# Local attention with global keys and a SwiGLU block: the written-out order of all steps replaced by another order

## Chip, core and metric

One core of one Trainium2 chip. The metric is the device time of one execution in microseconds, the median of several runs.

## The reference

Attention over `B, H, S, D = 4, 8, 768, 64`: a key is kept when it is one of the first 8 (global) or lies 0 to 95 positions back (local); a bias of a slope per head times the distance is added, then softmax. The result, 3072 tokens by 512, goes through a SwiGLU block.

```python
scores = scale * np.matmul(q, k.transpose(0, 1, 3, 2)) + bias
a = softmax(np.where(is_global | is_local, scores, -1e9))
x = (a @ v).transpose(0, 2, 1, 3).reshape(3072, 512)
g = x @ w_gate                       # 512 x 1536
out = (g * sigmoid(g) * (x @ w_val)) @ w_out
```

## The kernel before, in words

One Python string, `ORDER` (lines 67 to 147), names every step of the program with its arguments; the last lines of the kernel walk through it and call one function per step. There is no scheduler: each engine and each DMA queue executes its own steps in the order of the string, and semaphores hold a step until its inputs are there and its buffer is free. So a step's place in the string matters only against the steps of the same engine or queue, and for which buffers and PSUM banks it gets.

The 3072 tokens are four batches of two halves, eight token blocks `t = 2 * batch + half` of 384 tokens. Head pairs are numbered 0 to 3 (`hp`), two pairs make a group `g`. The steps that the text speaks of:

- **Software loads, issued by POOL** (lines 276 to 358), in a row: `Lh.i.half.h0.h1` heads of `k` (i = 0) or `q` (i = 1) of batch 0; `Lv.b.c` a chunk of 120 keys of the values (48 for c = 6); `Lr.b.i.h` one head of `k` or `q` as rows; `L4.i.h0` four heads; `Lw.which.n.g` half of a third of `w_gate` (0) or `w_val` (1), 256 KB; `Lo.g` a third of `w_out`, 512 KB; `Ld.P.half` distances for the masks. `Z.b.P` and `kz.P` are POOL memsets in the same row; `Z.b` clears parts of the value buffer, which two batches share in turn, and so waits for the last reader of the batch whose buffer it takes.
- **SP's queue**: a few early loads (`Lf.S`, `Li`, `Ld.S`); `D.b.hp.i` (line 483) transposes one head pair's rows by DMA into `kN` (i = 0) or `qT` (i = 1); `G.b...S` copies the global values; and the copies out that `e.t.i` issues (line 753).
- **PE**: `T` and `U` transposes, `b` and `B` bias products with a diagonal slope matrix, `C` and `c.b.g.half.up` scores (line 520), `V` and `W` weighted values (586, 614), `w` sums of weights (597, 630), `g.t.f` and `v.t.f` the four matmuls of one 128-wide slice `f` of gate and value product (line 693, both), `o.t.i.part` a quarter of one 128-token output tile (line 734; 723 for the last two tiles), `fill.n` matmuls whose result nothing uses (394).
- **ACT and DVE**: `cast`, `k`, `q`, `kw`, `qw`, `K` move and spread transposed keys and queries (the last letter is the engine); `E` and `x` exponentials (ACT); `M` masks from distances (ACT); `m` masking (DVE); `X` a copy of the values with the halves of the partitions swapped; `n` copies weighted values out of PSUM (ACT); `i`, `j`, `r`, `p` invert, spread and apply the sums, `p` writing the block's `xT`; `t` tanh (ACT), `s` and `h` the SwiGLU products (DVE, line 709); `e` scales an output tile by 0.5 on ACT (752) and issues its copy out.

Buffers that are handed on: eight PSUM banks, dealt in the order of the string from those released earliest (lines 236 to 259); two `osb` tiles for the copies out, so that `e` waits for the copy out two before it; two value buffers; two `kN`.

Batch 1's pairs 0 and 1 are transposed on PE (`U`), its pairs 2 and 3 by four `D` steps; batches 2 and 3 by eight `D` each.

Of the kernel before, what the change touches and what calls it, by code (L numbers as in the profile page):

```python
# [809 lines left out]
```

## Time and profile before

| | us |
|---|---|
| median of 3 runs (237.11 to 238.77) | 238.52 |
| the profiled execution's own time | 237.59 |
| its span, first to last instruction | 235.8 |
| PE busy in the span | 229.6 |
| DVE busy | 169.5 |
| ACT busy | 116.3 |
| POOL busy (issuing software loads, above all) | 79.8 |

The clock that was granted is 1.000. A row of the timeline has the start in the span, the length, the engine, the line of the kernel and the operation, with the output and input names; in brackets stands how long the engine sat idle ahead of it and what ended that. In the list of DMA issues the last number is the time from issue to landing. A row of the chain has start, length and what ran.

### The profile page before, as it was taken

To read this page: it belongs to the slowest core of one execution; us is meant where nothing else is said; L and a number is where in the kernel's file an instruction comes from. 1 tells how busy PE (TensorE), PEld (TensorE's weight loads), DVE (VectorE), ACT (ScalarE), POOL (GpSimd) and SP (SyncE) were. 2 spreads that over 40 slices of the span, in tenths; PEclk is the share of its full clock that TensorE was granted. 3 is DMA by queue.
4 is the path that set the end of the run, shared out by engine and by line. 5 is a ranking of instruction groups with operands and counts; after the bars stand their busy time and mean duration, and the time that the engine had idled before them with its cause. 6 is when DMAs were issued, how large, how long until landed. Compare 5 with 4: busy or idle time off the path is not lost.

```text
span 235.8 us, 6107 instructions
## 1 busy us (share of the span) xinstructions
PE 229.6 (97%) x2515; PEld 133.6 (57%) x2515; DVE 169.5 (72%) x389; ACT 116.3 (49%) x219; POOL 79.8 (34%) x113
## 2 busy tenths in 40 slices
PE   7999899998999999999999999999999999999998
PEld 4466566554455666655556556565555565555446
DVE  3998898869466789969979998984495876542200
ACT  3688847546842734357858674440424341311321
POOL 8976759731581599788100000000000000000000
DMA  6999999999999899999996311010012000010332
GB/s 171 194 180 188 204 197 178 171 140 122 188 145 184 190 161 135 124 153 153 143 204 152 39 49 47 0 47 0 3 44 89 0 3 0 1 44 3 135 129 93
DMA packets 88324, 25.97 MB, mean 110 GB/s; under 512 B 78048, under 2 KB 85256, under 8 KB 88296
## 3 DMA queue, kind: packets, MB, share of 16 engines
q0 software_dynamic: 67120, 14.25, 79.2%
q1 hardware_dynamic: 20488, 10.74, 23.4%
q10 hardware_dynamic: 688, 0.59, 0.7%
q8 instruction: 19, 0.31, 0.6%
q14 instruction: 9, 0.07, 0.1%
HBM read 28.93 MB, written 6.29 MB: 149 GB/s over the span
## 4 chain that ended last, share of the span: by engine, by line
PE 66%; DMA 23%; POOL 7%; ACT 3%; issue 1%; POOLq 0%; ACTq 0%
PE banks L693 39%; PE banks L734 20%; DMA kst<-in_k_dram 9%; DMA wo<-in_moe_w_out_dram 8%; DMA wv<-in_moe_w_val_dram 4%; DMA out_dram<-osb 2%; POOL vS L292 2%; PE banks L520 2%; PE banks L614 2%; PE banks L723 1%; PE banks L394 1%; POOL k L284 1%; POOL q L284 1%; POOL wg L351 1%; PE banks L630 1%
## 5 line engine op out<-in xcount | busy, mean ns | idle before, releaser
L699 ACT ACTIVATE th<-banks 128x384 f32<-128x384 f32 x96 | 44.3, 494 | 59.4 <-PE banks L693 56.4
L693 PE MATMUL banks<-xT,wv 128*128 128x384 f16 x384 | 71.4, 326 | 0.0
L693 PE MATMUL banks<-xT,wg 128*128 128x384 f16 x384 | 71.2, 326 | 0.1
L709 DVE TENSOR_TENSOR hT<-banks,sl 128x384 f16<-128x384 f32 x96 | 50.8, 552 | 21.2 <-PE banks L693 19.8
L734 PE MATMUL banks<-wo,hT 128*128 128x512 f16 x276 | 65.8, 379 | 0.0
L703 DVE SCALAR_TENSOR_TENSOR sl<-th,banks 128x384 f32<-128x384 f32 x96 | 50.1, 547 | 17.3 <-ACT th L699 16.7
L693 PEld LDWEIGHTS <-wv 128*128 128x128 f16 x384 | 37.3, 98 | 26.3
L693 PEld LDWEIGHTS <-wg 128*128 128x128 f16 x384 | 36.7, 98 | 25.6 <-issue 0.6
L734 PEld LDWEIGHTS <-hT 128*128 128x128 f16 x276 | 26.3, 98 | 28.2 <-issue 0.2
L530 ACT ACTIVATE at<-banks 128x976 f16<-128x976 f32 (+3 forms) x28 | 25.5, 958 | 12.1 <-PE banks L520 12.1
L292 POOL DMA_DIRECT2D vS<-in_v_dram x28 | 25.2, 908 | 9.8 <-DMA vS<-in_v_dram 6.7
L752 ACT ACTIVATE osb<-banks 128x512 f32<-128x512 f32 x23 | 13.5, 599 | 23.3 <-PE banks L734 14.6
L344 POOL DMA_DIRECT2D qst<-in_q_dram x20 | 17.2, 860 | 8.8 <-DMA wo<-in_moe_w_out_dram 4.1
L539 DVE TENSOR_TENSOR at<-at,masks 128x976 f16<-128x976 f16 (+3 forms) x26 | 15.7, 643 | 4.1 <-ACT at L530 4.1
L663 DVE STREAM_TRANSPOSE rb<-dR 128x384 f32<-128x384 f32 x32 | 16.7, 553 | 2.8 <-ACT dR L659 2.7
L344 POOL DMA_DIRECT2D kst<-in_k_dram x20 | 16.7, 841 | 2.6 <-DMA vS<-in_v_dram 1.1
L520 PE MATMUL banks<-qT,kT 64*64 64x152 f16 (+9 forms) x456 | 9.2, 214 | 1.6 <-DMA qT<-qst 1.6
L520 PEld LDWEIGHTS <-kT 64*64 64x64 f16 x456 | 7.2, 107 | 5.8 <-issue 4.8
L678 DVE TENSOR_TENSOR xT<-banks,rb 128x384 f16<-128x384 f32 x16 | 8.4, 546 | 1.3 <-PE banks L614 1.2
L319 ACT COPY vX<-vS 64x1792 f16<-64x1792 f16 (+2 forms) x6 | 7.3, 1220 | 3.3 <-DMA kst<-in_k_dram 3.2
L637 ACT COPY ns<-banks 128x768 f32<-128x768 f32 x6 | 4.7, 807 | 7.9 <-PE banks L614 7.9
L614 PEld LDWEIGHTS <-vS 64*64 64x64 f16 x228 | 6.6, 107 | 2.6 <-issue 2.1
(77 smaller groups left out, 165.2 us busy)
## 6 DMA issues: line engine op xcount, KB each, us to landing
out_dram<-osb SPq DMA_DIRECT2D x23, 256.0 KB, 2.1
vS<-in_v_dram POOLq DMA_DIRECT2D x24, 120.0 KB, 7.7
qst<-in_q_dram POOLq DMA_DIRECT2D x20, 96.0 KB, 7.2
kst<-in_k_dram POOLq DMA_DIRECT2D x20, 96.0 KB, 6.7
wg<-in_moe_w_gate_dram POOLq DMA_DIRECT2D x6, 256.0 KB, 7.3
wv<-in_moe_w_val_dram POOLq DMA_DIRECT2D x6, 256.0 KB, 8.2
wo<-in_moe_w_out_dram POOLq DMA_DIRECT2D x3, 512.0 KB, 18.2
k<-in_k_dram POOLq DMA_DIRECT2D x3, 192.0 KB, 5.7
```

The source lines that it names most:

```text
L292: nc.gpsimd.dma_start(out=v_of(b)[r0:r0 + n, c, heads(g), :], in_=v[b, heads(g), KC * c:KC * c + n, :].rearrange("h p d -> p h d"))
L344: nc.gpsimd.dma_start(out=rows_of(i, b, h // 2)[:, :, h % 2, :], in_=KQ[i][b, h].rearrange("(t p) d -> p t d", p=128))
L520: nc.tensor.matmul(sc[64 * r:64 * r + 64, hi, col:col + n], lhsT=kTs[2 * g + r][d, k0:k0 + 64], rhs=qTs[b, 2 * g + r][d, q0:q0 + n], start ...
L530: nc.scalar.activation(out=at[:, :, 0:w], in_=sc[:, :, 0:w], func=AF.Exp, scale=scale)
L539: ENG[e].tensor_mul(a2, a2, masks[:, 2 * g:2 * g + 2, x:x + w])
L663: nc.vector.transpose(rb.rearrange("p (n i) -> p n i", i=32), rbs[b, half][:, g, r].unsqueeze(2).broadcast_to([128, TB // 32, 32]))
L693: nc.tensor.matmul(gv[t, f, which][:, 0:TB], lhsT=w[:, c, 128 * f:128 * f + 128], rhs=xTs[t][:, c, :], start=(c == 0), stop=(c == NC - 1))
L699: nc.scalar.activation(out=th, in_=gv[t, f, 0][:, 0:TB], func=AF.Tanh, scale=0.5)
L703: nc.vector.scalar_tensor_tensor(out=sl, in0=gv[t, f, "t"], scalar=1.0, in1=gv[t, f, 0][:, 0:TB], op0=AluOp.add, op1=AluOp.mult)
L709: nc.vector.tensor_mul(hTs[t][:, f, :], gv[t, f, 1][:, 0:TB], gv[t, f, "s"])
L734: nc.tensor.matmul(ops_t[t, i], lhsT=hTs[t][:, f, 128 * i:128 * i + 128], rhs=wo[:, f, :], start=(f == 0), stop=(f == NFF - 1))
L752: nc.scalar.mul(out=osb, in_=ops, mul=0.5)
```

## The change

All steps stand in another order. The first fifteen software loads are the same ones in the same sequence, but for `Ld.P.1`, which stands two places earlier; from the sixteenth on the sequence differs. The scores (`c`) and DMA transposes (`D`) of batch 1, and nearly everything behind them, have other places among the products. Some copies move between ACT and DVE, three of the six `n` steps are gone, and the fillers are 5 + 10 at the start and 7 + 2 + 4 at the end instead of 11 + 5 and 23. No function is changed. Of the 80 lines on each side those that hold the steps spoken of:

```diff
--- before
+++ after
 ORDER = """
-Lf.A.1.1 Z.0.P pre Lf.S.0.1 Lf.A.1.0 cast.1.1.V Li cast.1.0.V fill.11 fill.5 Z.1.P kz.P sl.1 sl.7
-sl.6 cast.0.1.A T.1.0.1 Lh.0.0.4.8 T.1.0.0 Ld.S.2 sl.2 sl.0 sl.3 b.1.0 k.1.0.A Lh.1.0.4.8 Lf.S.0.0
-Lh.1.1.4.8 sl.5 T.0.0.1 b.1.1 q.1.0.V pk Ld.P.1 cast.0.0.A C.1.0 T.0.0.0 Lv.0.0 sl.4 Lh.0.1.0.4
...
-k.0.1.A q.1.1.V E.2.1 T.2.1.0 T.0.1.1 k.1.1.V q.2.1.V w.0.0.1 Lv.0.4 Lv.0.5 k.2.1.A B.1.1.0 q.0.1.A
-B.1.1.1 i.0.0.1 Lw.0.2.0 r.0.1.0.0 k.3.1.A V.1 c.0.0.1.0 p.0.0.0.1.V V.0 c.0.1.1.1 p.0.0.0.0.V V.2
-M.1.1 x.0.0.1.0 r.0.1.0.1 c.0.1.1.0 c.0.0.1.1 V.3 p.0.1.0.0.V p.0.1.0.1.V x.0.0.1.1 m.0.0.1.0.V
...
-t.0.11 s.0.11 p.0.1.1.1.V Lw.0.1.0 v.0.10 h.0.9 h.0.11 U.1.1 U.0.1 U.0.0 U.1.0 qw.1.A t.0.10 D.1.3.0
...
-g.1.11 kw.1.A t.1.0 D.1.2.1 g.1.3 s.1.2 h.0.10 v.1.2 v.1.10 s.1.0 h.1.0 h.1.2 Lr.1.0.4 v.1.3 t.1.3
-g.1.1 Lr.1.0.5 t.1.11 g.1.9 g.1.6 D.1.2.0 D.1.3.1 Z.2.P Lw.1.1.1 t.1.1 s.1.11 h.1.10 s.1.3 t.1.6
...
-s.1.9 c.1.0.0.1 Lv.1.0 s.1.8 s.0.6 x.1.0.0.0 x.1.0.0.1 Lv.1.2 h.1.1 h.1.8 Lo.0 g.0.7 g.1.7 g.0.5
-t.0.5 g.1.5 v.0.5 v.1.9 v.1.6 K.1.3 s.0.5 Lv.1.5 h.1.9 g.0.4 v.0.6 Lo.1 Lv.1.6 t.1.7 t.0.4 h.0.5
-h.1.6 c.1.0.1.0 v.1.7 t.0.7 Lo.2 s.1.7 s.0.4 h.0.6 Lv.1.4 Lv.1.3 t.1.5 x.1.0.1.0 s.1.5 g.1.4 Lv.1.1
...
-Lr.2.0.5 v.1.5 h.0.7 h.1.4 c.1.1.0.1 c.1.1.0.0 c.1.1.1.1 G.1.1.7.S x.1.1.0.1 x.1.1.0.0 h.1.5 o.0.0.0
-o.1.0.0 Lr.2.1.5 c.1.0.1.1 D.2.2.0 m.1.0.0.0.V c.1.1.1.0 x.1.1.1.1 M.3.0 Lr.2.1.7 Lr.2.0.6 o.0.0.1
...
-o.1.0.2 i.1.0 j.1.0.A o.1.2.1 o.0.2.1 i.1.1 Lr.2.0.2 Lr.2.1.4 r.1.1.0.0 Lr.2.0.1 e.0.0 o.1.0.3
-o.1.2.2 o.1.2.3 W.1.0.0 e.1.0 D.2.3.1 D.2.2.1 W.1.0.1 r.1.0.0.1 o.0.1.1 o.0.1.2 p.1.0.0.1.V
-p.1.1.0.0.V o.0.1.3 r.1.1.0.1 e.1.2 j.1.1.A r.1.0.0.0 p.1.1.0.1.V p.1.0.0.0.V o.0.2.2 o.0.2.3 g.2.3
-e.0.2 t.2.3 D.2.3.0 W.1.1.0 W.1.1.1 n.1.0.1 r.1.1.1.1 r.1.0.1.0 g.2.4 g.2.6 r.1.0.1.1 g.2.7 t.2.4
-v.2.6 Z.3.P s.2.3 s.2.4 n.1.1.1 g.2.1 g.2.2 t.2.6 t.2.2 Lr.3.0.6 Lr.3.1.6 p.1.0.1.1.V v.2.3 v.2.4
...
-e.6.0 o.7.1.2 h.7.9 o.7.1.3 o.7.2.0 e.6.1 o.7.0.1 e.7.1 o.7.0.2 o.7.0.3 o.7.2.1 o.7.2.2 o.7.2.3
-fill.23 e.7.0 e.7.3 e.7.2
...
+pre Z.0.P Lf.A.1.1 Lf.S.0.1 fill.5 Z.1.P Lf.A.1.0 kz.P Li cast.0.1.V cast.1.0.V cast.1.1.A fill.10
+sl.1 Lh.0.0.4.8 sl.2 Ld.P.1 sl.0 T.1.0.0 T.1.0.1 Ld.S.2 sl.3 T.0.0.1 k.1.0.A sl.4 q.1.0.A q.0.0.V
+b.1.1 Lf.S.0.0 Lh.1.0.4.8 sl.5 sl.7 cast.0.0.V b.1.0 Lh.1.1.4.8 C.1.1 Lv.0.0 C.1.0 E.1.1 Lh.0.1.0.4
...
+q.2.1.A c.0.0.1.1 i.0.0.1 V.1 V.2 V.0 Lw.0.2.0 r.0.1.0.1 Lv.0.5 B.1.1.1 M.0.1 p.0.0.0.0.V Lv.0.6
+p.0.0.0.1.V x.0.0.1.1 c.0.1.1.1 B.1.1.0 r.0.1.0.0 Lv.0.4 x.0.1.1.1 p.0.1.0.0.V V.3 c.0.0.1.0 Ld.P.0
...
+Lr.1.1.4 Lw.0.1.0 g.0.8 g.0.9 r.0.0.1.1 t.0.8 D.1.3.0 X.0.0.4.7.A s.0.1 s.0.8 r.0.0.1.0 r.0.1.1.0
...
+W.0.1.1 v.0.8 p.0.0.1.1.V p.0.0.1.0.V v.0.10 v.0.9 D.1.2.0 D.1.3.1 r.0.1.1.1 p.0.1.1.0.V v.0.11
...
+Z.3.P s.1.10 U.0.1 U.1.1 U.0.0 t.1.0 s.1.0 t.1.1 g.1.11 kw.1.V kw.0.A v.1.10 v.1.1 qw.0.A Lv.1.6
...
+g.0.6 h.1.0 v.1.11 s.1.8 g.1.9 s.1.2 Lv.1.1 M.0.0 g.1.6 h.1.2 Lw.1.1.1 h.1.3 t.1.9 g.0.5 s.1.9
+Lr.2.1.3 h.1.11 c.1.0.0.0 t.0.6 t.0.5 t.1.6 s.0.6 c.1.0.0.1 x.1.0.0.1 D.1.2.1 v.1.8 Lv.1.5 g.1.4
+s.1.6 g.0.7 g.0.4 h.1.8 s.0.5 v.1.9 v.0.6 Lr.2.0.4 Lv.1.0 t.0.7 x.1.0.0.0 s.0.7 M.3.0 h.1.9 K.1.3
+Lo.0 Lo.1 g.1.7 t.0.4 v.1.6 c.1.0.1.0 h.0.6 t.1.7 s.0.4 s.1.7 v.0.7 Lo.2 Lr.2.0.0 h.1.6 v.1.4 Lv.1.2
...
+h.0.5 c.1.1.1.1 Lr.2.1.2 c.1.1.0.0 x.1.0.1.0 c.1.1.0.1 s.1.5 h.1.5 M.2.1 o.0.1.0 o.0.2.0 x.1.1.1.1
+x.1.1.0.1 o.0.0.0 Lr.2.0.7 M.2.0 m.1.1.1.1.V o.1.2.0 Lr.2.1.5 Lr.2.1.4 G.1.1.7.S Lr.3.1.2 o.0.0.1
+m.1.0.0.0.V Lr.2.0.6 o.1.2.1 x.1.1.0.0 c.1.0.1.1 c.1.1.1.0 o.0.2.1 o.0.0.2 x.1.1.1.0 o.0.1.1 o.1.2.2
...
+W.1.0.0 o.0.2.3 e.0.0 r.1.1.0.0 Lr.2.0.2 r.1.0.0.0 D.2.3.0 o.1.0.0 e.0.2 p.1.0.0.1.V Lr.2.0.5
+o.1.0.1 p.1.1.0.0.V r.1.1.0.1 j.1.1.A D.2.2.1 p.1.0.0.0.V p.1.1.0.1.V o.1.0.2 o.1.0.3 e.1.2 Lr.2.1.6
+g.2.1 g.2.2 r.1.1.1.1 r.1.1.1.0 g.2.6 g.2.3 g.2.4 Lr.2.1.7 t.2.1 r.1.0.1.0 D.2.2.0 v.2.1 e.1.0 t.2.2
+v.2.6 s.2.1 s.2.2 D.2.1.1 t.2.3 D.2.3.1 t.2.4 s.2.3 g.2.0 v.2.4 s.2.4 h.2.1 t.2.6 t.2.0 s.2.6
+W.1.1.0 h.2.6 W.1.1.1 Z.2.P v.2.3 Lr.3.1.7 s.2.0 p.1.1.1.1.V e.0.1 p.1.1.1.0.V g.2.9 r.1.0.1.1
...
+h.7.10 o.7.1.2 o.7.1.3 o.7.0.1 e.6.0 o.7.2.0 o.7.0.2 o.7.0.3 o.7.2.1 e.5.0 o.7.2.2 o.7.2.3 fill.7
+e.5.1 e.7.1 fill.2 e.7.0 e.7.3 fill.4 e.7.2
 """
```

More of the change, by code (lines that the diff above doesn't have):

```diff
@@ new lines @@
+g.2.5 v.3.8 h.3.1 s.2.8 g.3.0 Lv.2.3 t.2.10 g.3.2 t.2.5 D.2.0.1 s.3.8 c.2.1.1.0 s.2.10 Lr.3.0.7
+t.3.0 s.2.5 s.3.0 c.2.1.1.1 Lr.3.1.4 v.2.8 v.2.10 x.2.1.1.1 g.3.11 v.3.2 x.2.1.1.0 Lv.2.0 t.3.2
+h.3.8 g.3.4 h.2.8 h.2.10 t.3.11 s.3.2 Lr.3.1.0 v.3.0 Lv.3.2 s.3.11 Lv.2.6 Lv.3.0 v.2.5 h.3.2 g.3.6
+Lv.3.4 o.2.2.0 o.2.1.0 h.3.0 K.2.1 m.2.1.1.1.V g.3.7 t.3.6 t.3.4 s.3.6 h.2.5 Lr.3.0.6 s.3.4
+c.2.1.0.0 c.2.1.0.1 x.2.1.0.1 o.2.2.1 o.2.2.2 t.3.7 G.2.1.7.S K.2.0 Lv.2.5 o.2.2.3 Lr.3.1.1 v.3.11
+x.2.1.0.0 c.2.0.1.1 c.2.0.1.0 s.3.7 g.3.3 x.2.0.1.0 m.2.1.0.1.V h.3.11 o.2.1.1 o.2.1.2 Lv.3.5 Lv.3.3
@@ new lines @@
+c.2.0.0.1 x.2.0.1.1 m.2.1.1.0.V t.3.3 m.2.0.1.0.V Lr.3.0.4 m.2.0.1.1.V m.2.1.0.0.V Lr.3.0.5
+c.2.0.0.0 x.2.0.0.1 o.2.1.3 o.1.1.0 g.3.10 g.3.5 x.2.0.0.0 t.3.10 e.2.1 Lr.3.1.6 Lr.3.1.5
+m.2.0.0.1.V D.3.3.1 Lv.2.1 Lv.2.4 D.3.2.0 e.2.2 o.2.0.0 m.2.0.0.0.V Lv.3.6 w.2.1 w.2.0 s.3.10 t.3.5
+X.2.1.0.7.V s.3.5 o.1.1.1 D.3.2.1 o.2.0.1 X.2.0.0.7.A i.2.0 Lr.3.0.1 D.3.3.0 v.3.4 v.3.6 j.2.0.A
+o.1.1.2 i.2.1 D.3.0.1 h.3.4 G.3.1.7.S o.2.0.2 r.2.1.0.1 o.2.0.3 h.3.6 o.1.1.3 e.2.0 r.2.1.0.0
+Lr.3.0.0 W.2.0.1 W.2.0.0 s.3.3 W.2.1.1 r.2.0.0.0 Lr.3.0.2 p.2.1.0.0.V v.3.5 p.2.1.0.1.V v.3.3
@@ new lines @@
+t.4.10 p.2.0.1.0.V m.3.1.0.1.V p.2.1.1.1.V c.3.0.0.0 s.4.10 t.4.4 g.4.2 x.3.0.0.0 s.4.4 g.5.4 g.5.1
+m.3.0.0.1.V v.4.4 x.3.0.1.1 m.3.1.1.0.V h.4.6 v.4.10 o.3.0.0 o.3.0.1 t.5.4 t.4.2 t.4.5 m.3.0.0.0.V
+o.3.0.2 v.4.5 Lv.3.1 m.3.0.1.1.V m.3.0.1.0.V s.4.5 h.4.10 v.4.2 s.4.2 s.5.4 X.3.1.0.7.A w.3.0
+X.3.0.0.7.A w.3.1 h.4.5 W.3.0.1 h.4.2 o.3.0.3 i.3.0 j.3.0.A t.5.1 o.3.2.0 i.3.1 r.3.1.0.1 g.5.6
+h.4.4 s.5.1 j.3.1.A o.3.2.1 o.3.2.2 o.3.2.3 e.3.0 W.3.1.0 r.3.1.0.0 p.3.1.0.1.V W.3.1.1 p.3.1.0.0.V
+W.3.0.0 r.3.0.0.0 e.3.2 n.3.1.1 v.5.4 g.5.10 v.5.1 n.3.0.1 v.5.10 t.5.10 r.3.0.0.1 p.3.0.0.0.V
@@ new lines @@
+p.3.0.0.1.V t.5.6 v.5.6 g.6.6 h.5.4 g.5.5 t.6.6 h.5.1 s.5.10 s.5.6 v.4.0 g.4.0 v.6.6 h.5.10 t.4.0
+g.5.9 g.5.3 r.3.1.1.1 s.6.6 h.5.6 t.5.5 s.4.0 v.5.5 r.3.1.1.0 g.5.0 h.6.6 r.3.0.1.0 g.5.11 s.5.5
+t.5.9 t.5.11 t.5.3 g.4.7 h.5.5 h.4.0 s.5.11 s.5.9 g.4.9 g.6.7 g.6.11 v.5.9 v.5.11 t.4.7 s.5.3 t.6.7
+s.4.7 g.6.4 s.6.7 v.5.3 t.4.9 h.5.9 h.5.11 t.6.4 v.4.7 v.6.7 s.4.9 p.3.1.1.1.V v.4.9 g.6.1 h.6.7
+t.6.1 g.5.7 h.4.7 h.4.9 h.5.3 v.6.1 s.6.4 p.3.1.1.0.V v.6.4 t.5.7 t.6.11 s.6.1 g.6.10 g.6.3 s.5.7
+o.4.0.0 v.6.10 s.6.11 o.4.0.1 h.6.4 t.6.10 h.6.1 r.3.0.1.1 g.5.2 t.5.2 g.6.0 v.5.7 s.6.10 s.5.2
@@ new lines @@
+h.7.8 h.7.4 g.7.3 g.7.9 g.7.2 o.6.2.2 o.6.1.3 t.7.3 t.7.9 s.7.1 o.5.2.0 t.7.0 s.7.3 s.7.9 g.7.10
+v.7.3 t.7.2 t.7.10 h.7.1 v.7.0 s.7.0 s.7.2 o.5.2.1 o.5.2.2 o.5.0.0 o.5.0.1 e.6.1 o.5.0.2 o.6.0.0
+v.7.2 h.7.3 h.7.0 o.5.2.3 o.5.1.0 h.7.2 g.7.7 o.6.2.3 o.5.1.1 o.6.0.1 o.6.0.2 t.7.7 v.7.10 o.6.0.3
+e.5.2 o.7.1.0 e.6.2 o.5.0.3 o.5.1.2 s.7.10 v.7.7 v.7.9 s.7.7 o.7.1.1 o.7.0.0 h.7.9 h.7.7 o.5.1.3
+h.7.10 o.7.1.2 o.7.1.3 o.7.0.1 e.6.0 o.7.2.0 o.7.0.2 o.7.0.3 o.7.2.1 e.5.0 o.7.2.2 o.7.2.3 fill.7
+e.5.1 e.7.1 fill.2 e.7.0 e.7.3 fill.4 e.7.2
```

87 lines of the change are left out of this document (29 added, 58 removed).

## The prediction

> **What bounds the kernel now.** I read the page first, then the stretches of the span, then the matrix engine's own timeline and the chain of work that ended last.
>
> ```profile
> PE 229.6 (97%) x2515; PEld 133.6 (57%) x2515; DVE 169.5 (72%) x389; ACT 116.3 (49%) x219; POOL 79.8 (34%) x113
> ...
> PE 66%; DMA 23%; POOL 7%; ACT 3%; issue 1%; POOLq 0%; ACTq 0%
> ```
> ```profile
> 50.00:60.00 10.00, 8.44 (x107) 5.05 (x107) 8.23 (x19) 4.73 (x10) 2.20 (x3) 1.00 1.61 133
> ...
> 120.00:130.00 10.00, 10.00 (x118) 5.87 (x117) 9.09 (x24) 6.53 (x10) 0.00 (x0) 1.00 0.83 171
> ```
> Columns after the length: PE, PEld, DVE, ACT, POOL, clock, DMA share, GB/s. From 80 us on every stretch of PE but the last is full like the second row; behind the head, the stretch 50 to 60 is the one with the largest hole, and DMA moves only 133 GB/s in it.
>
> ```profile
> 16.40 1.01 PE L504 MATMUL banks<-dist,slopeI 128*128 128x488 f16 x4
> 17.34 0.72 PE L586 MATMUL banks<-at,vS 128*64 128x216 f16 x8
> 18.00 0.42 PE L520 MATMUL banks<-qT,kT 64*64 64x128 f16 x20
> ...
> 20.45 2.33 PE L693 MATMUL banks<-xT,wg 128*128 128x384 f16 x12
> ...
> 24.23 0.24 PE L630 MATMUL banks<-at,pick 128*32 128x112 f16 x5 [0.82 <-issue]
> ...
> 59.43 0.78 PE L520 MATMUL banks<-qT,kT 64*64 64x160 f16 x40 [1.56 <-DMA qT<-qst]
> ...
> 60.17 1.47 PE L734 MATMUL banks<-wo,hT 128*128 128x512 f16 x6
> ...
> 77.20 0.24 PE L614 MATMUL banks<-at,vS 64*64 64x128 f16 x2 [0.35 <-ACT osb L752]
> ```
> ```profile
> 232.15 2.67 PE L394 MATMUL banks<-ones 128*128 128x256 f16 x23
> ```
> ```profile
> 164.14 3.90 PE banks L693 x24
> ...
> 210.90 2.59 PE banks L734 x12
> ```
> So the first product `g` starts at 20.45 and the last matmul of the result ends at about 232.15: 211.7 us in which PE waits 0.82 + 1.56 + 0.35 = 2.73. A product (four matmuls) takes 3.90 / 6 = 0.65, an output part 2.59 / 4 = 0.65. Both orders hold the same matmuls behind the first `g`, so the new time is the old one plus what changes at four places: the head; the point near 60 us, where `c.1.1` waits for its transposes and the first output part for `wo`; batch 1's end; and the tail. Up to the first `o` both orders also hold the same matmuls: all products of blocks 0 and 1, and at the last the three `c.1.1` scores.
>
> **The head.** Of the first software loads only the mask distances `Ld.P.1` have moved, two places forward, which sets two `q` loads back by one load; of the casts and evacuations that change engine, three `q` copies leave DVE for one cast and one `k` that come. These lie in front of a later wait: the head ends with the `V` steps, and these need the value chunk of `Lv.0.2`, whose place is the same.
>
> ```profile
> 9.04 2.81 POOL L292 DMA_DIRECT2D vS<-in_v_dram  x3
> ```
> ```profile
> vS<-in_v_dram POOLq DMA_DIRECT2D x2, 120.0 KB, 7.0
> ```
> The third of these loads is issued near 10.9 and lands 7 us later, at 17.8, inside the first `V`. Before, both `B` steps (the L504 row, 1.0) were done ahead of it, and from 18.0 to 20.45 three `V` and four scores stood in front of the first `g`. After, one score (some 0.4) goes ahead and both `B` come behind: 2.45 + 1.0 - 0.4 = 3.05, and `g` starts near 21.1. Price +0.7; bounds 0, if the two `B` find a wait to hide in, and +1.0, if the score doesn't get ahead. The 0.82 at 24.2 has no releaser and I leave it as it is.
>
> **Transposes of batch 1, and `wo`.**
> ```profile
> 39.73 1.35 SPq L483 DMA_TRANSPOSE qT<-qst  x1
> ...
> 44.87 4.38 SPq L483 DMA_TRANSPOSE qT<-qst  x1
> ```
> ```profile
> qT<-qst SPq DMA_TRANSPOSE x1, 8.5
> ```
> ```profile
> qT<-qst SPq DMA_TRANSPOSE x1, 14.5
> ```
> ```profile
> wo<-in_moe_w_out_dram POOLq DMA_DIRECT2D x1, 512.0 KB, 17.1
> vS<-in_v_dram POOLq DMA_DIRECT2D x1, 120.0 KB, 14.7
> ```
> ```profile
> 40.35 1.86 POOL L292 DMA_DIRECT2D vS<-in_v_dram  x2
> 42.19 0.79 POOL L356 DMA_DIRECT2D wo<-in_moe_w_out_dram  x1
> ```
> ```profile
> 44.29 18.16 DMA wo<-in_moe_w_out_dram
> ```
> The fourth transpose lands at 44.87 + 14.5 = 59.4, which ends the 1.56. `Lo.0` lands at 42.19 + 17.1 = 59.3, just ahead of the first `o`. The change puts `Lv.1.6` (48 KB), `Lv.1.1`, `Lv.1.5` (120 each) and `Lr.2.1.3` (96) ahead of `Lo.0` and takes `Lv.1.2` (120) away: 264 KB more, which at the 133 GB/s of that stretch are 2.0 us. `Lo.0` then lands near 61.3. The third and fourth transposes (now `q` of head pairs 3 and 2) need `Lr.1.1.7` and `Lr.1.1.5`, which come one 256 KB weight load further down the row: 1.9 at that rate, of which some falls into the time in which the third stood behind the second anyway. I take half, 1.0: the fourth lands at 60.4, and the three scores take 0.75 (59.43 to 60.17). PE comes to the first of these scores at 59.43 - 1.56 + 0.7 = 58.6, so the head's 0.7 lies inside this wait; if the wait went, it would show. First `o` at 61.3 against 60.17: price **+1.1**. Next is `Lo.1` (before: 44.29 + 18.16 = 62.45), now at 63.5, since one of the added loads was ahead of it already; the fifth output part needs it first, at 61.3 + 4 x 0.65 = 63.9. So nothing more is late there. The price's lower bound is that neither is late: PE's own work alone, 60.17 - 1.56 + 0.7 = 59.3, or -0.9; the upper one is the second rival.
>
> The Trainium skill, "DMA: Bandwidth & Descriptors", section "SWDGE vs HWDGE vs iDMA", has each DMA engine take turns between the queues that software and hardware feed. By that rule alone a transpose is late by what its issue is late, the whole 1.9, and the first `o` would start at 62.0; an estimate, 0.7 above mine. The 8.5 and 14.5 neither bear it out nor speak against it.
>
> **Batch 1's end.** On SP the output copies now alternate with the transposes of batch 2: `e.0.2`'s copy stands behind `D.2.3.0`, which waits for `Lr.2.0.6`.
> ```profile
> 67.61 0.84 POOL L344 DMA_DIRECT2D kst<-in_k_dram  x1
> ...
> 78.54 0.68 POOL L309 MEMSET vS<- 32x256 uint32 x2 [6.78 <-ACT dR L659]
> ```
> ```profile
> kst<-in_k_dram POOLq DMA_DIRECT2D x1, 96.0 KB, 4.8
> ```
> ```profile
> out_dram<-osb SPq DMA_DIRECT2D x1, 256.0 KB, 5.0
> ```
> ```profile
> 76.55 0.60 ACT L752 ACTIVATE osb<-banks 128x512 f32<-128x512 f32 x1 [4.60 <-DMA out_dram<-osb]
> ```
> That load landed at 67.61 + 4.8 = 72.4; two more 96 KB loads ahead of it make 73.8. Its transpose takes 1.35 of SP's time, the copy out 5.0: 80.2. Only then has ACT a buffer for `e.1.0` (0.6), and behind that on ACT wait `t.2.2`, `t.2.3`, `t.2.4` and `t.2.6`, for whose banks the next products and `W.1.1` wait. PE reaches `v.2.6` at 61.3 + 16.7 (60.17 to 77.20 less the 0.35, one product in it) + 5 more products x 0.65 = 81.2. I expect some 0.8 of waiting in place of 0.35: **+0.5**, bounds -0.35 (none) and +3 (that transpose as slow as the 8.5). `W.1.1` comes eight products later, so POOL's clear of the value buffer, which needs it done, goes from 78.54 to about 85, and the last loads with it. That costs nothing under its cover: 32 loads remain behind it instead of 34, and their first scores, `c.2.0`, come no earlier than before:
> ```profile
> 107.85 0.60 PE L520 MATMUL banks<-qT,kT 64*64 64x152 f16 x28
> ```
> Without that cover the 6.5 us would show. Three `n` copies dropped, and `X`, `kw` and `j.3.1` on other engines, change work that PE isn't waiting for.
>
> **The tail.** Fillers go from 23 to 13, 2.67 / 23 = 0.12 each.
> ```profile
> SPq L805 <- PE banks L394: 0.6, 1, 0.6
> ```
> SP's closing waits end on the fillers, 0.6 behind everything else. Ten fewer end 1.2 earlier, and the last output decides: **-0.5** (bounds 0 and -0.6). The output copies of blocks 5 to 7 have another order, but each finds its bank and buffer free when its last part is done.
>
> **Sum.** 1.1 + 0.5 - 0.5 = +1.1. The profiled execution took 237.59 (span 235.8) and would take 238.7; the median of the runs is 238.52, and on it the forecast is **239.6**. Within 1%, 236.1 to 240.9, is about what a measurement of this kernel can't tell from no change.
>
> **The rivals.** *Earlier (0.22).* The two `k` transposes now go first, so the `q` ones may meet a quieter queue: no wait at 58, none at 77, no loss in the head: -1.56 - 0.35 - 0.5 = -2.4, 236.1; without the 0.82 as well, 235.3. For it: with 133 GB/s in that stretch it isn't bandwidth that makes them late. Against: more bytes stand ahead of `Lo.0`.
>
> *A weight late (0.20), the slower side.*
> ```profile
> 38.13 1.39 POOL L351 DMA_DIRECT2D wv<-in_moe_w_val_dram  x2
> ```
> ```profile
> wv<-in_moe_w_val_dram POOLq DMA_DIRECT2D x2, 256.0 KB, 7.0
> ```
> Before, `Lw.1.1.1` and `Lw.1.1.0` had landed by 38.8 + 7.0 = 46. Now `Lw.1.1.1` stands behind two more value loads, near where `Lv.1.2` took 14.7 us (41.3 to 56.0) with a transpose beside it. PE needs it at `v.0.6`, ten products and four scores ahead of the first `o`, 6.5 + 1.2 = 7.7: at 59.3 - 7.7 = 51.6, if nothing else waits. I put its landing at 46 + 168 KB / 133 GB/s + some 3 = 50. It decides from a landing after 61.3 - 7.7 = 53.6; at 56.0 the first `o` starts at 63.7, 3.5 late: 238.52 + 3.5 + 0.5 - 0.5 = 242.0. For it: the 14.7. Against: that load was one of several, and the one before it took less.
>
> *Copies behind transposes (0.10).* The +3 above in place of the +0.5: 242.1.
>
> *Nothing of it counts (0.05).* All is absorbed as it is now and only the fillers show: 238.0.
>
> **How the numbers follow.** The forecast has 0.43. Faster by over 1% is the part of the first rival in which one more of the small waits goes, 0.14; slower by over 1% are the second and third, 0.30; the other 0.56 lies between. The range reaches from the first rival, 236.1, to 242.8, the two slower ones with some margin.
>
> **What would show it.** Right: first L693 matmul near 21.1; first L734 matmul near 61.3, with a PE wait for `qT` or `wo` just ahead; a PE wait near 82 while ACT's `osb` waits for a copy out; POOL's clear near 85; no PE gap from 90 on; 13 fillers that end before the last output lands. Wrong: a first L734 before 59.5 (the DMA queue wasn't the limit), a PE wait for `wv` near 52, or gaps after 100.

## The result, and the profile after

The kernel after takes 236.21 us (median of 8 runs, 235.79 to 237.34), the one before 237.64 in the runs beside it (8 runs, 237.03 to 238.77): a ratio of 0.9942, 95% interval 0.9914 to 0.9971. So it is 0.6% faster, where 239.6 was forecast, 0.5% slower than the 238.52 shown; 236.21 lies just inside the range. The profiled execution took 236.86 with a span of 235.1; before it was 237.59 and 235.8. In both kernels single executions lie some 1 us around their median, so profiles are compared place by place, and medians for the whole. Ratios leave out executions that took over 1.5% more than the fastest of their kernel (five of e5's twelve, one or two elsewhere).

The page's line of busy times, the chain of work that ended last, and the two stretches around 50 us, after:

```profile
PE 228.1 (97%) x2504; PEld 132.2 (56%) x2504; DVE 166.8 (71%) x385; ACT 117.0 (50%) x220; POOL 79.1 (34%) x113
```
```profile
PE 65%; DMA 23%; POOL 6%; DVE 3%; issue 1%; ACT 0%; SPq 0%; DVEq 0%; POOLq 0%; ACTq 0%
```
```profile
40.00:50.00 10.00, 10.00 (x88) 5.97 (x87) 7.55 (x16) 7.01 (x14) 6.55 (x9) 1.00 2.05 146
50.00:60.00 10.00, 8.68 (x110) 5.27 (x109) 8.12 (x21) 6.35 (x10) 5.06 (x7) 1.00 1.61 144
```

PE is as full as before, the chain has nearly the same make-up, and the hole between 50 and 60 is still there: 8.68 of 10 busy instead of 8.44. DMA moves 144 GB/s in it instead of 133. PE's timeline after, at the places that the prediction names:

```profile
21.12 2.77 PE L693 MATMUL banks<-xT,wg 128*128 128x384 f16 x16
23.83 0.64 PE L630 MATMUL banks<-at,pick 128*32 128x128 f16 x36
...
58.26 0.82 PE L520 MATMUL banks<-qT,kT 64*64 64x160 f16 x44 [0.68 <-DMA qT<-qst]
59.71 4.13 PE L734 MATMUL banks<-wo,hT 128*128 128x512 f16 x18 [0.64 <-DMA wo<-in_moe_w_out_dram]
...
82.78 0.24 PE L614 MATMUL banks<-at,vS 64*64 64x128 f16 x2 [0.37 <-DVE hT L709]
...
231.88 1.58 PE L394 MATMUL banks<-ones 128*128 128x256 f16 x13
```

The first product starts at 21.12, as forecast. The step `w.0.1` is one row of 36 matmuls, without the 0.82 of before. The wait of 1.56 for `qT` has become 0.68 for `qT` and 0.64 for `wo`, and the first `o` starts at 59.71, where 61.3 was forecast and 60.17 was before. These two rows of DMA issues, at 48.19 and 48.34, say when the two landed:

```profile
wo<-in_moe_w_out_dram POOLq DMA_DIRECT2D x1, 512.0 KB, 11.3
qT<-qst SPq DMA_TRANSPOSE x1, 10.0
```

The fourth transpose lands at 58.2 (before 59.4) and `Lo.0` at 59.7 (before 59.3), in spite of the 264 KB more ahead of it. From the first `o` to the fillers it is 172.17 (before 171.98), and from the fillers' start to the end of the span 3.2 (before 3.65).

### The profile page after: what moved, and what is told of

The parts are those of the page before. It is cut to its first block, busy times and chain, and to the rows that moved or that the text cites. A ratio compares the mean times of both kernels' runs of the same rounds, so it can differ in the third digit from the quotient of the medians.

```text
span 235.1 us, 6093 instructions
## 1 busy us (share of the span) xinstructions
PE 228.1 (97%) x2504; PEld 132.2 (56%) x2504; DVE 166.8 (71%) x385; ACT 117.0 (50%) x220; POOL 79.1 (34%) x113
## 4 chain that ended last, share of the span: by engine, by line
PE 65%; DMA 23%; POOL 6%; DVE 3%; issue 1%; ACT 0%; SPq 0%; DVEq 0%; POOLq 0%; ACTq 0%
PE banks L693 39%; PE banks L734 20%; DMA vS<-in_v_dram 6%; DMA kst<-in_k_dram 5%; DMA wv<-in_moe_w_val_dram 4%; DMA qst<-in_q_dram 4%; DMA k<-in_k_dram 3%; PE banks L614 2%; PE banks L520 2%; POOL vS L292 1%; DMA out_dram<-osb 1%; PE banks L723 1%; POOL qst L344 1%; POOL q L284 1%; PE banks L630 1%
## 5 line engine op out<-in xcount | busy, mean ns | idle before, releaser
L693 PEld LDWEIGHTS <-wv 128*128 128x128 f16 x384 | 36.8, 98 | 26.3 <-DMA wv<-in_moe_w_val_dram 0.7
L693 PEld LDWEIGHTS <-wg 128*128 128x128 f16 x384 | 37.2, 98 | 25.5 <-DVE xT L678 0.2
L530 ACT ACTIVATE at<-banks 128x1008 f16<-128x1008 f32 (+3 forms) x28 | 25.7, 957 | 10.6 <-PE banks L520 9.6
L539 DVE TENSOR_TENSOR at<-at,masks 128x1008 f16<-128x1008 f16 (+3 forms) x26 | 16.2, 645 | 5.3 <-ACT at L530 4.9
L678 DVE TENSOR_TENSOR xT<-banks,rb 128x384 f16<-128x384 f32 x22 | 11.0, 542 | 1.0 <-PE banks L614 0.8
L319 ACT COPY vX<-vS 64x1792 f16<-64x1792 f16 (+2 forms) x7 | 9.0, 1287 | 3.3 <-DMA vS<-in_v_dram 3.1
L614 PE MATMUL banks<-at,vS 64*64 64x152 f16 (+9 forms) x228 | 8.0, 213 | 0.4 <-DVE hT L709 0.4
```

Source lines behind the costliest of these rows:

```text
L530: nc.scalar.activation(out=at[:, :, 0:w], in_=sc[:, :, 0:w], func=AF.Exp, scale=scale)
L539: ENG[e].tensor_mul(a2, a2, masks[:, 2 * g:2 * g + 2, x:x + w])
L614: nc.tensor.matmul(num[64 * hi:64 * hi + 64, r, q0 - HB * half:q0 - HB * half + n], lhsT=vSs[b][k, c, h] if up == r else crossed[b][k, c, ...
L693: nc.tensor.matmul(gv[t, f, which][:, 0:TB], lhsT=w[:, c, 128 * f:128 * f + 128], rhs=xTs[t][:, c, :], start=(c == 0), stop=(c == NC - 1))
```

## The experiments

Four sets were run, each with the kernel before beside it on the same chip. In all of them the two numbers to look at are when the fourth transpose of batch 1 lands and when the first `o` starts. "Bytes" is the theory of the prediction: a load lands by what stands ahead of it, at the rate of that stretch. The rivals are named with each.

**The two kernels again, and the tail alone.** `e1_before_again`:

> The kernel before, unchanged, for a second profile. Theory P (the transposes of batch 1 set the point near 60 us): the fourth transpose lands at 59.4 +- 0.5 again, with a PE wait of 1.2 to 2 ahead of c.1.1, first L734 matmul at 60.2 +- 0.5. Theory N (that landing is chance): it moves by more than 1 us. The 0.82 wait without releaser in w.0.1 either recurs (it belongs to the place in the stream) or not (chance).

`e2_after_again`:

> The changed kernel, unchanged, for a second profile and as the base of the others of this call. Theory P: first L734 matmul again at 59.7 +- 0.5, ratio to before 0.994 +- 0.003. Theory N: first L734 anywhere from 58.5 to 61.5. No wait without releaser in w.0.1 if that belongs to the place in the stream.

`e3_tail13` is the order before with one edit:

```diff
-fill.23 e.7.0 e.7.3 e.7.2
+fill.13 e.7.0 e.7.3 e.7.2
```

> The kernel before with 13 fillers at the end in place of 23, nothing else. My step on the tail: -0.45 us (0.2%), the last output's landing ends the span. Rival (the fillers don't hold the end): 0.

Before again: first `o` at 60.61 behind a wait for `qT` of 2.3 (a little more than expected), the fourth transpose at 59.8, `w.0.1` with 0.6 inside. After again: first `o` at 59.77 behind 0.8 for `qT` and 1.4 for `wo`, the fourth transpose at 57.5, `Lo.0` at 59.7, no wait in `w.0.1`; median 236.26, ratio 0.9946 (0.992 to 0.9973). So what the first pair of profiles shows repeats. With 13 fillers the tail is 3.24 instead of 3.65, as SP then waits for the copy out alone (0.9, no row for the fillers); of 237.21 against 237.42, 0.9992 (0.9963 to 1.0021), the timed runs can't tell that. The tail gives 0.4 in the profiles, and the rest of the 0.7 between the two profiles comes from elsewhere.

**Does a later PE move the first `o`?** `e4_delay8` is the order after with 8 fillers, 0.87 us (23.66 to 24.53), behind the third `g`:

```diff
+fill.8 g.0.2
-g.0.2
```

> The changed kernel with 8 more fillers among the first products, 0.87 us of PE work more at 23 us. Theory P (PE waits for DMA at 58 to 60 anyway): first L734 unmoved at 59.7, the total moves by less than 0.3. Rival (PE is the bound from the first product on): +0.87, first L734 at 60.6.

PE's timeline in it, at the first `o` and at a wait behind the `o` steps that the order after hadn't had:

```profile
58.38 0.82 PE L520 MATMUL banks<-qT,kT 64*64 64x160 f16 x44
59.30 4.06 PE L734 MATMUL banks<-wo,hT 128*128 128x512 f16 x18
...
80.57 0.81 PE L693 MATMUL banks<-xT,wv 128*128 128x384 f16 x4 [1.45 <-ACT osb L752]
```

The first `o` started at 59.30, not later than without the fillers. PE ends its scores at 59.2 and `Lo.0` lands at 46.60 + 12.7 = 59.3, so the 0.87 filled the waits that the order after has there (0.68 and 0.64) and cost nothing. What PE gains or loses ahead of the first `o` (the head's 0.7, the 0.82 in `w.0.1`) is absorbed as long as such a wait is left. But the median went to 237.60 (0.9998, 0.997 to 1.0027), 1.3 more than after, where less than 0.3 was expected; the wait of 1.45 fits that. It is the third rival, copies out behind transposes on SP, and it needs little to show.

**What makes the transposes late?** Four kernels on one chip. `e5_wo_early` puts the loads of `wo` in the order after back ahead of the small loads; `e6_wo_late` does the change's part with the loads alone in the order before; `e7_k_first` does the part with the transposes alone:

```diff
# e5, POOL's row in the order after (slots kept)
-Lv.1.6 Lv.1.1 Lw.1.1.1 Lr.2.1.3 Lv.1.5 Lr.2.0.4 Lv.1.0 Lo.0 Lo.1 Lo.2
+Lw.1.1.1 Lr.2.0.4 Lv.1.0 Lo.0 Lo.1 Lo.2 Lv.1.6 Lv.1.1 Lr.2.1.3 Lv.1.5
# e6, POOL's row in the order before
-Lr.2.0.4 Lv.1.0 Lv.1.2 Lo.0 Lv.1.5 Lo.1 Lv.1.6 Lo.2 Lv.1.4 Lv.1.3 Lv.1.1 Lr.2.1.6 Lr.2.1.3
+Lv.1.6 Lv.1.1 Lr.2.1.3 Lv.1.5 Lr.2.0.4 Lv.1.0 Lo.0 Lo.1 Lo.2 Lv.1.2 Lv.1.4 Lv.1.3 Lr.2.1.6
# e7, order before: the row loads, and SP's transposes
-Lr.1.1.5 Lr.1.1.4 Lr.1.0.4 Lr.1.0.5
+Lr.1.0.5 Lr.1.0.4 Lr.1.1.4 Lr.1.1.5
-D.1.2.1 D.1.2.0 D.1.3.1
+D.1.2.0 D.1.3.1 D.1.2.1
```

> The order after, with the three loads of wo put ahead of Lv.1.6, Lv.1.1, Lr.2.1.3 and Lv.1.5 in POOL's row, as they stood before the change; nothing else moves. Bytes (the prediction's theory: wo lands by what stands ahead of it at 133 GB/s): Lo.0 lands near 57.5 instead of 59.7, the fourth transpose stays at 57.5 to 58.2, the first o goes to about 59.0, and the time falls by 0.6 to 235.6. Neighbours (transposes are slow while wo moves beside them): the third and fourth transposes land later again, the fourth at 59.4 to 59.9, the first o starts at 60.1 to 60.6 with a wait for qT of 1.5 to 2.3, and the time goes up by 0.5 to 236.8.

> The order before, with Lv.1.6, Lv.1.1, Lr.2.1.3 and Lv.1.5 put ahead of the three loads of wo, as the change has them; nothing else moves. Bytes: Lo.0 lands near 61.3, the first o starts there with a wait for wo, and the time goes up by 1.0 to 238.4. Neighbours: the third and fourth transposes land earlier, the fourth near 58, the first o starts at 59.5 to 59.8, and the time falls by 0.4 to 237.0. Order (which of k and q goes first decides, and not wo): the fourth transpose stays at 59.3 to 59.9, and with it the first o and the time.

> The order before, with batch 1's transposes in the order of after (k of both pairs first) and the four 96 KB row loads that feed the last three put in that order too; wo stays where it was. Order: the fourth transpose lands near 58, the first o starts near 59.6, held by Lo.0 at 59.3, and the time falls by 0.5 to 236.9. Neighbours: the fourth transpose stays at 59.3 to 59.9, the first o at 60.1 to 60.6, and the time within 0.3 of before.

| | fourth transpose issued, landed | `Lo.0` issued, landed | first `o` | span | ratio to before (95%) |
|---|---|---|---|---|---|
| before | 44.87, 59.4 | 42.19, 59.3 | 60.17 | 235.8 | 1 |
| after | 48.19, 58.2 | 48.34, 59.7 | 59.71 | 235.1 | 0.9942 (0.9914 to 0.9971) |
| e5, `wo` early | 48.52, 62.7 | 40.87, 54.5 | 64.06 | 239.5 | 1.0096 (1.005 to 1.0142) |
| e6, `wo` late | 44.81, 54.3 | 44.81, 57.6 | 58.12 | 233.0 | 0.9868 (0.9832 to 0.9905) |
| e7, `k` first | 43.60, 53.0 | 42.12, 55.0 | 58.12 | 233.0 | 0.9883 (0.9844 to 0.9923) |

All three go against bytes. In e6 `Lo.0` has 264 KB more ahead of it, is issued 2.6 later, and lands 1.7 earlier. Issued at nearly the same time as before, the fourth transpose lands 5 us earlier. In e5 it lands 4.5 later than in the order after, with the same transposes. Neither "neighbours" nor "order" had said how much: both of the edits, made alone in the order before, take the whole wait away, which none had expected. In the profiles of e6 and e7 no wait of PE is listed from 30 us to the fillers, and the first `o` starts where PE itself gets to it.

The reason can be counted. Here are the rows of two queues in a stretch of 4 us, software loads (`q0`) and the queue of the transposes (`q1`); the columns are packets, MB, and the share of 16 DMA engines (the shares overlap). First e7, where the transposes run beside value and row loads, then e5, where they run beside `wo`:

```profile
q1 hardware_dynamic: 1620, 0.40, 82.5%
q0 software_dynamic: 1697, 0.20, 82.3%
```
```profile
q0 software_dynamic: 629, 0.63, 92.0%
q1 hardware_dynamic: 633, 0.15, 29.9%
```

In both the queues move equally many packets: they take turns. (So it is in the order before from 50 to 53, 387 and 383. Where the counts differ, as in the order after from 52 to 54 with 1068 and 660, it isn't shown that both queues had work on every engine.) A packet of a transpose has 0.40 MB / 1620, some 256 bytes. One of a value or row load has 0.20 / 1697, some 128, and one of `wo` 0.63 / 629, some 1024. Beside the small ones the transposes get 405 packets in a microsecond, beside `wo` 158. A transpose is 768 rows of 128 numbers of two bytes, 192 KB or 768 packets: at these rates, as an estimate, 1.9 us beside values and 4.9 beside a weight. And e5's stretch moves 0.78 MB, e7's 0.60: the stretch with more GB/s is the one in which the transposes are slow, so the rate of bytes says nothing of when they land.

The two orders themselves fit this. In the order before, from 48.27 to 55.25, the loads' packets have 400 bytes on average (0.62 MB in 1550), and the transposes move 1241 packets in 6.98 us; after, from 48.34 to 54.49, they have 134 bytes (0.49 MB in 3649), and it is 1330 in 6.15 us. But turns aren't the whole of it. In the order after, from 54.49 to 58.21, the two rows are:

```profile
q0 software_dynamic: 434, 0.42, 117.7%
q1 hardware_dynamic: 270, 0.06, 50.0%
```

There a packet of a transpose is busy for 0.500 x 16 x 3.72 us / 270 = 110 ns, against 30 in e5's rows (0.299 x 16 x 4 us / 633), and one of `wo` for 161 against 94. Something else slows both queues in that stretch, and in the order before from 55.25 to 59.4 too (100 ns for a transpose's packet). What it is, no run shows.

The Trainium skill, "DMA: Bandwidth & Descriptors", section "Queues, rings and completion order", has each DMA engine go from queue to queue and serve one packet of each. The equal counts agree; in the Trainium skill a packet holds several descriptors, and whether a packet in these rows is one such isn't shown. The prediction used the same rule for the issue of a transpose and left out what follows from it: the length of a turn is set by the other queue's packet.

e5 lost more than its `qT` wait explains by itself: its span is 4.4 longer than that of the order after, and its wait of 5.07 stands in place of 0.68 and 0.64, 3.75 more. The clock's part in that is taken up below.

**The packets by themselves.** `e10_wo_packets` leaves the order before as it is and cuts each load of `wo` into four of 128 columns:

```diff
-        nc.gpsimd.dma_start(
-            out=wo[:, 4 * g:4 * g + 4, :],
-            in_=moe_w_out[512 * g:512 * g + 512].rearrange("(f p) d -> p f d", p=128))
+        for c in range(0, DM, 128):
+            nc.gpsimd.dma_start(
+                out=wo[:, 4 * g:4 * g + 4, c:c + 128],
+                in_=moe_w_out[512 * g:512 * g + 512, c:c + 128].rearrange(
+                    "(f p) d -> p f d", p=128))
```

> The order before, with each load of wo cut into four of 128 columns, so that it moves in packets of 256 bytes instead of 1024; the bytes and the order are the same, and POOL issues nine loads more (0.8 each). Packets: the third and fourth transposes land at 53 to 57 instead of 55.3 and 59.4, PE's wait for qT shrinks under 0.5 and what is left of it is for wo, whose first third lands between 57.5 and 60; the time is the same to 1.5 lower. Bytes: the transposes stay at 55 and 59.4 with a wait for qT of 1.5 to 2.3, and the time is the same or, by POOL's extra issues, higher.

PE's timeline in it, then the two queues between 53 and 54 and the fourth transpose, issued at 44.80:

```profile
57.35 0.82 PE L522 MATMUL banks<-qT,kT 64*64 64x160 f16 x44
58.54 1.46 PE L736 MATMUL banks<-wo,hT 128*128 128x512 f16 x6 [0.37 <-DMA wo<-in_moe_w_out_dram]
```
```profile
q0 software_dynamic: 333, 0.08, 82.9%
q1 hardware_dynamic: 327, 0.08, 64.1%
```
```profile
qT<-qst SPq DMA_TRANSPOSE x1, 10.5
```

With the same bytes in the same order the fourth transpose lands at 55.3 instead of 59.4, the wait for `qT` is gone, and beside packets of 256 bytes the transposes get 327 in a microsecond, between the 158 and the 405. So it is the size of the neighbour's packets that sets the transposes' rate. The time hardly follows (237.65; 0.9963, 0.9933 to 0.9992): smaller packets make `wo` itself slower, PE waits 0.37 and 0.36 for it, and 1.13 for a copy out at 76.9. From the first `o` to the fillers it is 173.9 instead of 172.0: the gain of 1.6 at the first `o` was given back.

**Batch 1's end.** `e8_copies_first`, the order after with three transposes moved on SP:

```diff
-r.1.0.0.0 D.2.3.0 o.1.0.0 e.0.2
+r.1.0.0.0 o.1.0.0 e.0.2
-j.1.1.A D.2.2.1 p.1.0.0.0.V
+j.1.1.A p.1.0.0.0.V
-r.1.0.1.0 D.2.2.0 v.2.1 e.1.0 t.2.2
+r.1.0.1.0 v.2.1 e.1.0 t.2.2
-s.2.1 s.2.2 D.2.1.1
+s.2.1 s.2.2 D.2.3.0 D.2.2.1 D.2.2.0 D.2.1.1
```

> The order after, with three transposes of batch 2 (D.2.3.0, D.2.2.1, D.2.2.0) put behind the copies out of e.0.2, e.1.2 and e.1.0 on SP. Copies (ACT's waits for osb, 1.8 at 76.7 and 0.9 at 78.6, hold the tanh steps, and the 0.4 that PE waits for hT ahead of W.1.1.1 comes from there): both osb waits shrink under 0.7, PE's wait near 82 goes, and the time falls by 0.4 to 235.8. Rival (the DVE is behind by itself): the wait near 82 stays and the time is within 0.2 of after; and if the later transposes hold POOL's loads, gaps show behind 95 and the time goes up.

ACT's waits for `osb` from 70 to 84 go from 2.8 to 1.4, and the 0.37 ahead of `W.1.1.1` is gone. From the first `o` to the fillers it is 171.58 (after: 172.17 and, again, 172.24). The median is 235.92, 0.9909 (0.9874 to 0.9945), against 0.9942 for after: the intervals overlap, so the 0.6 is shown in the profile and not in the time. That profile's first `o` is at 58.51 with nothing moved ahead of it, which is how much one execution differs from another here.

**Can the order after be mended the same way?** In it the two row loads of the last two transposes stand behind a weight, so that these are issued at 45.81 and 48.19 instead of 43.4 and 44.9. `e9_rows_first` moves the rows ahead, `e12_rows_copies` has the edit of e8 as well, `e14_rows_w` in addition a value weight:

```diff
# e9, e12, e14
-Lw.1.1.0 Lr.1.1.7 Lr.1.1.5
+Lr.1.1.7 Lr.1.1.5 Lw.1.1.0
# e14
-Lv.1.6 Lv.1.1 Lw.1.1.1
+Lw.1.1.1 Lv.1.6 Lv.1.1
```

> The order after, with the two row loads Lr.1.1.7 and Lr.1.1.5, which feed the third and fourth transposes of batch 1, put ahead of the weight load Lw.1.1.0. Packets (a transpose and the loads take turns packet by packet, so that a transpose beside the 1024-byte packets of a weight is slow and beside the 128-byte packets of rows and values is quick): the third and fourth transposes are issued 1.3 to 1.9 us earlier, run beside value loads alone, the fourth lands at 54 to 56.5, Lo.0 at 58 to 59, the first o starts at 58 to 59.2, and the time falls by 0.5 to 1.5 against after, to 235. Bytes: Lo.0 has the same bytes ahead and stays at 59.7, the first o there too, and the time does not move from 236.3.

> The order after, with the two row loads ahead of Lw.1.1.0 and three transposes of batch 2 behind the copies out of e.0.2, e.1.2 and e.1.0, both edits together. If each does its part (first o at 58 to 59.2, no wait near 82), the profiled span is 233 to 233.6 and the median 234.8 to 235.3, as low as the order before with k first. If the rows bring nothing, 235.9.

> The order after with the two row loads ahead of Lw.1.1.0, then Lw.1.1.1 ahead of Lv.1.6 and Lv.1.1, and three transposes of batch 2 behind the copies out of e.0.2, e.1.2 and e.1.0. If the late weight was what held the row loads' gain back: Lw.1.1.1 lands before 48.5, no wait for wv, the fourth transpose lands at 55 to 57, the first o starts at 58.3 to 59.3, span 233.3 to 234.2, median 235.2 to 235.8 where before is 237.7. If the transposes are slow again beside the weight that now stands with them: the fourth at 58 or later, the first o at 59.7, and no gain on after (236.3).

In e9 the fourth transpose lands at 55.1, inside what packets gave, and yet the first `o` is at 60.05. The row of the value weight, issued at 40.44, and what PE does:

```profile
wv<-in_moe_w_val_dram POOLq DMA_DIRECT2D x1, 256.0 KB, 12.1
```
```profile
52.57 0.50 PE L693 MATMUL banks<-xT,wv 128*128 128x384 f16 x2 [1.96 <-DMA wv<-in_moe_w_val_dram]
```

`Lw.1.1.1` lands at 52.5 and PE waits 1.96 for it: the second rival, at its place and at a smaller price (that rival had a landing at 56.0, and the first `o` 3.5 late). That the early transposes take their turns from this weight fits, and is not counted here. The time is that of after (236.88; 0.9943, 0.9914 to 0.9973). In e12 the weight happened to land at 49.4 and the first `o` was at 58.36, but from there to the fillers it is 173.1, with a wait of 0.7 for the next third of `wo` in it, and the median doesn't move either (236.73; 0.9944). With the weight ahead, e14, its profile has the transposes slow again, beside both weights (10.5 and 12.9 for the first two), `Lo.0` at 61.0 and a wait of 2.49; its times spread from 235.61 to 240.12 (median 237.50; 0.9971, 0.9934 to 1.0008). That profile is the slowest of its runs and shows what goes wrong there, not its typical time. So the order after can't be mended by its loads alone in any way tried: rows, weights and transposes want the same 15 us, and PE needs the weight soonest.

**The wait inside `w.0.1`, and the best of both.** `e11_w_later` is e7 with one step moved; `e13_both_before` has the edits of e6, e7 and e3 together.

```diff
# e11
-m.0.0.1.1.V w.0.1 X.0.0.2.4.A X.0.1.2.4.V g.0.0
+m.0.0.1.1.V X.0.0.2.4.A X.0.1.2.4.V g.0.0 w.0.1
```

> The run with k first, and there the weights step w.0.1 put one product later (behind g.0.0). Instruction fetch (the 0.6 to 0.8 inside w.0.1 is PE running out of instructions, as a fetch of 16 KB that starts near 21.6 comes too late for it): PE gets to that instruction 0.65 later, the wait shrinks to 0.2 or less, and as no wait lies behind it in that run the time falls by 0.5, to 234.9 at the median. Rival (the wait belongs to the step, by data that the profile does not name): it stays 0.6 inside w.0.1, and the time does not move.

> The order before with wo's loads behind the value loads, with k first among batch 1's transposes, and with 13 fillers at the end instead of 23. Packets: no wait is left at the scores or at the first o, as in either edit alone, so the first o starts near 58.1 and the two edits do not add up (PE's own work is the limit, with the 0.6 inside w.0.1 in it); the tail gives 0.4: profiled span 232.6, median 234.8 where before is 237.7.

In e11 the wait is gone from `w.0.1`, but PE then stands as long one product further on:

```profile
24.01 0.78 PE L630 MATMUL banks<-at,pick 128*32 128x128 f16 x36
26.37 2.27 PE L693 MATMUL banks<-xT,wv 128*128 128x384 f16 x12 [0.83 <-DVE sl L703]
```

Its bank is freed by DVE later than the product now comes. The time stayed (235.81; 0.9893, 0.9859 to 0.9928). So the wait doesn't belong to the step's data, and taking it away alone is worth nothing; that it is an instruction fetch is not shown by this. e13 came out at 235.02, 0.9875 (0.9837 to 0.9912): the two edits don't add up, as expected, and the tail, 3.2 in its profile, doesn't show in the median (that profile, span 234.1, is the slowest of its runs; 232.6 was expected). e6, at 235.15, and e13 are the fastest versions run, 1.3% below before and, by intervals that don't touch, below after.

## Why the prediction was wrong

| place | forecast | profiles, after less before |
|---|---|---|
| head, inside a later wait | +0.7 | +0.67 (20.45 to 21.12), absorbed |
| 0.82 in `w.0.1` | 0 | -0.82, absorbed |
| first `o` | +1.1 | -0.46 (60.17 to 59.71); again, -0.84 (60.61 to 59.77) |
| first `o` to the fillers | +0.5 | +0.19 (171.98 to 172.17) |
| fillers to the end | -0.5 | -0.4 (3.65 to 3.2) |
| span | +1.1 | -0.7 |

**The step that failed** is "Transposes of batch 1, and `wo`", and in it the sentence "264 KB more, which at the 133 GB/s of that stretch are 2.0 us". Its +1.1 was -0.5 to -0.8. The other two terms of the sum were right to 0.3, and they add up to nothing: the sign of the forecast hung on this one. Two things were wrong in it. The 133 GB/s was read as the rate that loads get. It is a mean over 10 us in which slices of 0.2 us (50 to 58) go from 13 to 234; and the same two queues together move 195 beside `wo` (e5) and 150 beside values (e7), with the transposes slow in the first and quick in the second. So bytes divided by such a rate don't say when a load or a transpose lands. And the transposes were priced by what their issue loses. After the change the third and the fourth are issued 2.4 and 3.3 later, and the fourth still lands 1.2 earlier, as more of its turns are beside values and fewer beside `wo`. `Lo.0`, behind more bytes, loses only 0.4; that the transposes are done with sooner fits this, but no run tries it apart from the rest.

The first rival had the right sentence ("with 133 GB/s in that stretch it isn't bandwidth that makes them late") and ended at the right time, 236.1, but by a quieter queue for the `q` transposes, a full 1.56 and the 0.35. The waits did not go: 1.32 is left after, and 0.37 in place of the 0.35. That its number fits is luck: it was counted from 238.52, a median of 3 runs, and from the 237.64 of 8 runs it would have been 235.2 (and the forecast 238.7). It is e6 and e7 that do what this rival says, and the order before does it too, with one half of the change.

**The 0.82** was left as it is; it went. It doesn't count in these two orders, as a wait for DMA is left behind it in both; e4 shows that for 0.87.

**Batch 1's end** was right in place and direction: PE waits near 82.8 for `hT`, which comes from tanh steps behind an `osb` that waits for a copy out; with the copies ahead (e8) it is gone. Its size, 0.2 for 0.5 (0.4 in the second pair, 171.86 to 172.24), is what is left when the wait at 77.2 goes. e4 shows the larger price of the third rival, 1.45, from the same mechanism. **The tail** was right (0.4 for 0.5). POOL's clear came at 83.7 (forecast 85) and cost nothing; from 90 on PE has no gap.

What stays open: why the medians differ by 1.4 and the two pairs of profiles by 0.7 and 0.9 only, so that the table accounts for about half of the change; which part of the 0.7 the smaller moves of the change have (three `n` fewer, copies on other engines), as none was tried alone; what ends the wait in `w.0.1`; what slows both queues from 55 to 58; and why single executions of one order differ by a microsecond at the first `o` (the last section has a part of it).

## What to carry to other kernels

Where DMA transposes share the engines with loads, ask what each transpose has beside it, not how many bytes stand ahead: a large-packet weight next to a transpose delays the transpose, and the transpose delays the weight. Put the small-packet loads beside the transposes and the weights behind them, and see that the weight which PE needs first isn't the one that pays. And before a stall is priced, find what sets the next fixed point: in the orders before and after, what PE gained or lost ahead of the first `o` went into a wait there, while in e6 and e7, where no wait is left, PE itself sets that point.

## What the runs showed of the hardware

**A wait can cost the clock as well.** Behind e14's wait of 2.49 the granted clock is half, and the output parts run at half speed; columns as in the stretches above, the clock is the third from the end:

```profile
58.00:60.00 2.00, 0.52 (x39) 0.36 (x27) 0.95 (x3) 1.84 (x3) 2.00 (x3) 1.00 1.27 204
60.00:62.00 2.00, 0.99 (x3) 0.44 (x4) 1.41 (x3) 1.59 (x2) 1.32 (x2) 0.50 1.24 210
62.00:64.00 2.00, 2.00 (x7) 0.63 (x5) 0.77 (x2) 0.00 (x0) 0.10 (x1) 0.50 1.24 213
64.00:66.00 2.00, 2.00 (x6) 0.74 (x5) 0.00 (x0) 0.00 (x0) 0.82 (x1) 0.50 1.48 189
66.00:68.00 2.00, 2.00 (x15) 0.74 (x17) 0.00 (x0) 0.00 (x0) 0.55 (x1) 0.79 2.39 154
```

PE starts again at 61.0 and has half the clock until 66.8: 2.9 us lost, more than the wait itself. e5 shows the same behind its wait of 5.07 for `qT` (0.50 from 64 to 66); the order before, with a wait of 2.27 in its second profile, kept 1.00. So in this kernel a wait near 2.5 us is worth removing for two reasons. The Trainium skill, "TensorE: Matmul & The Clock Gate", section "What's actually happening", puts the edge at an idle window of about 3.4 us. Here 2.49, with 0.8 of scores and 0.61 of waiting ahead of it, was enough, and the measurement decides.

The clock also goes with the spread of one order's times. Of 91 executions of the order before in the four sets (without two that took 596 and 820 us), 26 had a mean granted clock of 0.993 instead of 1.000, and they took 238.7 on average where the other 65 took 237.5. Of the 20 executions of the order after 2 had less than 1.000, of the 24 of e6, e7, e11 and e13, whose profiles show no wait for `qT`, none, and of e5's twelve all. A mean of 0.993 over 236 us is, as an estimate, 3.3 us at half the clock. None of the 26 was profiled, so that it is the wait for `qT` that costs them the clock isn't shown.

**All DMA can stand nearly still.** In the order before, between 50 and 53 us, in forty slices of 75 ns:

```profile
GB/s 162 181 183 164 155 160 159 176 362 169 152 148 143 172 159 167 159 130 119 133 147 79 85 96 89 44 75 10 14 3 14 17 72 145 210 152 149 190 159 185
...
q8 instruction: 1, 0.02, 1.9%
```

For some 0.4 us almost nothing moves. One packet of the instruction queue (some 16 KB: the profile's page has 19 of them with 0.31 MB) starts in the slice with 362, at 50.6 to 50.7, and is busy for 0.9 us (1.9% of 16 engines over 3 us), so the hole begins some 0.4 us behind its end. The order after and e6 have such a hole from 51.4 to 52.2 and from 51.2 to 52.1, with such a packet ahead of it as well; e7 has the packet and no hole. It was not tried whether that packet is the cause.
